# Decoding double-precision weights by one integer addition, with loads in the output weights' space and another opening order

## The chip, the cores and the metric

The kernel runs on one core of a Trainium2 chip. A core has a matrix engine (TensorE, PE in the profile), three engines for elementwise work (VectorE = DVE, ScalarE = ACT, GpSimd = POOL) and a queue that issues the loads and stores (SyncE = SP). Each engine executes its own list of instructions strictly in order; an instruction that waits holds up everything listed behind it on that engine. The metric is the device time of one execution in microseconds (us), the median of several.

## What is computed

Three stages follow one another: a packed attention, a block with softmax-weighted units and a layer norm, and a maximum of three products.

```python
q, k, v: (8, 8, 576, 64)    p: (8, 8, 32, 64)        # batch, heads, tokens, width
p_packed = sm_attn(p, k, v)                          # 32 packs per head
out      = sm_attn(q, p_packed, p_packed)            # tokens attend to the packs
x        = out as (4608 tokens, 512)
h   = x @ w_in                                       # (4608, 1024)
s   = h * softmax(h);   ln = (s - mean) / sqrt(var + 1e-6) * g_ln
x   = ln @ w_out                                     # (4608, 512)
h   = maximum(x @ w1, x @ w2, x @ w3)                # (4608, 768)
out = h @ w_out2                                     # (4608, 512)
```

The matrices w_in, w_out, w1, w2, w3 and w_out2 arrive as 64-bit floating point. The kernel reads each number as two 32-bit words, high and low, and makes a 32-bit float of them on the chip: this is the decoding that the change is about.

## The kernel before

**Tiles.** Tokens go in 36 tiles of 128 (the code's t), and four tiles make a block of 512. The attention of one batch is packed first: its keys are turned and scored against the packs (steps K and s), exponentiated (e), summed and inverted (i), turned (E), and multiplied into the values (p, t). The packed values times w_in give a matrix M of 1024 columns, kept as a high and a low part Mh and Ml (step M, two halves of 512 columns). The queries are turned (Q), and the tokens' shares in the packs are computed in two units per batch (x scores and exponentiates on DVE and ACT, a divides, turns back and splits into ah and al). A tile's h is then ah and al times Mh and Ml: 6 matmuls of 512 columns per half and batch part (steps a and b of `hidden_parts`, lines 649 to 720), followed by a maximum and an exponential (x), the product h * e with its square (c), and the scaling (d). Four such tiles are transposed 128 columns at a time (step T, `y_transpose`) and multiplied by w_out (step y, 6 matmuls per step). Results go to memory, and from about 520 us on the last stage takes them up again. Products of full precision are three matmuls each, of high and low parts.

**Decoding.** `decode` (line 120) works on a raw tile of 512 or 256 numbers per partition. `start` scales the high word on ACT into a scratch tile dt (line 131). `first_half` is two DVE instructions: shift and mask dt (136), and put the sign back into the high word (139). `second_half` is two more on DVE, which cut out the exponent (144) and multiply the low word by it (146), and one addition on POOL (149). There are 8 pieces of w_in, 4 + 8 of w_out (named raw, dt, wt, woh, wol) and 48 of the other matrices, which are decoded along the way, one piece at a time.

**What sets the order.** The opening is written out by hand: the string `st` in `CFG` lists the steps, and `manual_schedule` (line 1117) keeps every engine's list in that order. In it a capital L loads a piece of w_in, 1, 2 and 3 are the three parts of its decoding, o loads a piece of w_out, 4 to 7 are its parts, H0a to H3d are the steps of the first four tiles, and a leading b marks the second batch's steps. From tile 4 on a loop issues steps by the strings s0 to s3, and the program's scheduler interleaves them. Loads wait for the space that they fill: a tile of a pool is taken again only when its last reader is done.

Of the kernel before, what the change touches and what calls it, by code (L numbers as in the profile page):

```python
# [8 lines left out]
F32 = mybir.dt.float32  # L9
# [10 lines left out]
def f32(ap):  # L20
    return ap.bitcast(F32)
# [29 lines left out]
    l0='vv',  # L51
    wr=3,
    l1='v',
# [3 lines left out]
    d0='gggg',  # L57
    fs='g',
    d1='g',
    d2='g',  # L60
# [5 lines left out]
def kernel(  # L66
# [47 lines left out]
    make_identity(nc, ident)  # L114

# [4 lines left out]
    def decode(dst, raw, t, t2=None, add=nc.gpsimd, parts=False):  # L120
# [22 lines left out]
        def second_half():  # L143
            nc.vector.tensor_scalar(t.bitcast(I32), hi, -0x800000, None, op0=ALU.bitwise_and)
            if t2 is None:
                nc.vector.scalar_tensor_tensor(  # L146
                    out=f32(lo), in0=lo.bitcast(U32), scalar=2.0 ** -52, in1=t, op0=ALU.mult, op1=ALU.mult
                )
                add.tensor_tensor(out=dst, in0=f32(hi), in1=f32(lo), op=ALU.add)  # L149
            else:  # L150
                nc.gpsimd.tensor_tensor(out=t, in0=t2, in1=t, op=ALU.mult)
                add.tensor_tensor(out=dst, in0=f32(hi), in1=t, op=ALU.add)
# [32 lines left out]
    woh = big.tile([P, KFF, DM], F32R, name="woh")  # L185
    wol = big.tile([P, KFF, DM], F32R, name="wol")
# [16 lines left out]
    def decode_w_in(c, n):  # L203
        ns = slice(n * 512, (n + 1) * 512)
        raw = wide(words(w_in)[c * P:(c + 1) * P, ns, :])
        t = lt_p.tile([P, TB], F32, tag="ll", name="dt")
        t2 = lt_p.tile([P, TB], F32, tag="lh", name="dt2") if CFG['l0'][n] == 'g' else None
        return [*decode(w_in_sb[:, c, ns], raw, t, t2, parts=True)]
# [4 lines left out]
    def decode_w_out(n, raw):  # L213
# [3 lines left out]
        start, bits, product = decode(wt, raw, t, wt if CFG['l1'] == 'g' else None, ENG[CFG['d1']], parts=True)  # L217
# [23 lines left out]
    def decode_piece(src):  # L241
# [7 lines left out]
        return wt, *decode(wt, raw, t, add=ENG[CFG['d2']])  # L249
# [61 lines left out]

    def split(hi, lo, ps):
        nc.scalar.copy(hi, ps)
        nc.vector.tensor_tensor(out=lo, in0=ps, in1=f32(hi), op=ALU.subtract)
# [27 lines left out]
    class Packed:  # L342
# [145 lines left out]
        def product(self, n):  # L488
# [5 lines left out]
            mp = [bank("mp") for _ in range(NG)]  # L494
# [6 lines left out]
            for g in range(NG):  # L501
                split(Mh[b][:, g, ns], Ml[b][:, g, ns], mp[g])
# [68 lines left out]
        def run(self, what):  # L571
# [3 lines left out]
                K=[self.keys], E=[self.weights], V=[self.values, self.turned_values], M=[self.product], Q=[self.queries],  # L575
# [3 lines left out]
            for x, n in zip(what[::2], what[1::2]):  # L579
                for f in do[x]:  # L580
                    f(int(n))
                self.done.add({'a': 'X'}.get(x, x) + n)
# [4 lines left out]
    class First(Packed):  # L587
# [21 lines left out]
        def room_e1(self, g):  # L609
            if g == 0 or self.b:  # L610
                return super().room_e1(g)
            return [lt_p.tile([P, TB], F32, tag="lh", name="e1")[:, :HALF] for _ in range(2)]

# [423 lines left out]
    def start_step(w):  # L1037
        if w == 'L':
# [295 lines left out]
```

## Time and profile before

| | |
|---|---|
| median of 3 runs | 1087.29 us (1087.15 to 1088.55) |
| the profiled execution | 1090.56 us, of which its span is 1088.8 us |
| PE busy | 1034.7 us, 95% of the span |
| DVE busy | 725.7 us, 67% |
| ACT busy | 475.8 us, 44% |
| POOL busy | 268.0 us, 25% |

An engine's busy share is an average over stages. In the page's table of 40 slices PE is busy 5 to 8 tenths in the first four (27 us each) and 9 tenths in all but one of the rest, so the opening is the place where the matrix engine waits most. The clock that PE is granted has two levels, 1.00 (2.4 GHz) and 0.50 (1.2 GHz); a row between them holds some of both. What ended an idle time is named behind an arrow.

### The profile page before, as it was taken

The numbers are of one execution on the slowest core, as the hardware profiler recorded it, in microseconds if no ns is written. First come the engines' busy times: TensorE is split into PE (matmuls) and PEld (weight loads), VectorE is DVE, ScalarE is ACT, GpSimd is POOL, SyncE is SP. The second block draws the span as 40 slices with busy tenths as digits, with TensorE's granted clock in tenths as the row PEclk, the third lists the DMA queues.
The fourth block names the chain that finished last, engine by engine and source line by source line (L and its number), as shares of the span: only waits on it lengthen the run. The fifth ranks groups of instructions, "written<-read, shape, count | busy, mean of one in ns | idle before, by whom it ended". The sixth has DMA issues, their size and how long they took to land.

```text
span 1088.8 us, 18024 instructions
## 1 busy us (share of the span) xinstructions
PE 1034.7 (95%) x6548; PEld 871.2 (80%) x6548; DVE 725.7 (67%) x1454; ACT 475.8 (44%) x925; POOL 268.0 (25%) x291
## 2 busy tenths in 40 slices
PE   5788999999999999999999999999999999999997
PEld 3355757676777767777899999999989999999996
DVE  5979797878779786764878736725745663672560
ACT  5484867665766666566333421321231142132112
POOL 1214211110212121142577511320140042031002
PEclk9689999999999999999999999999999999999999
DMA  9751537455364643247564644543544453433311
GB/s 270 173 144 57 141 95 207 138 148 158 108 174 118 180 124 106 69 141 240 165 211 165 201 139 123 143 158 116 151 141 146 126 179 120 118 117 125 119 56 59
DMA packets 139464, 154.28 MB, mean 142 GB/s; under 512 B 51824, under 2 KB 92272, under 8 KB 139376
## 3 DMA queue, kind: packets, MB, share of 16 engines
q1 hardware_dynamic: 139376, 153.14, 47.5%
q8 instruction: 52, 0.85, 0.4%
q14 instruction: 36, 0.29, 0.1%
HBM read 116.92 MB, written 36.18 MB: 141 GB/s over the span
## 4 chain that ended last, share of the span: by engine, by line
PE 51%; DVE 2%; issue 1%; POOL 1%; DMA 1%; ACT 1%; DVEq 0%; ACTq 0%; POOLq 0%
PE m L953 32%; PE o L1224 13%; PE y L794 4%; PE h L682 1%; DVE wt L853 1%; DVE r L961 0%; PE tp L765 0%; DVE kept L961 0%; POOL w2l L826 0%; DMA wt<-wdram 0%; DMA wt<-wodram 0%; ACT u L718 0%; POOL hl L1017 0%; POOL t1l L921 0%; DVE t L903 0%
## 5 line engine op out<-in xcount | busy, mean ns | idle before, releaser
L794 PE MATMUL y<-lh,woh 128*128 128x512 f32 x288 | 118.8, 417 | 0.7 <-ACT lh L771 0.7
L794 PE MATMUL y<-ll,woh 128*128 128x512 f32 x288 | 115.8, 402 | 0.2 <-DVE ll L772 0.2
L794 PE MATMUL y<-lh,wol 128*128 128x512 f32 x288 | 114.6, 398 | 0.4 <-POOL wol L222 0.4
L961 DVE TENSOR_TENSOR u<-m,q 128x384 f32<-128x384 f32 x54 | 30.0, 555 | 126.6 <-PE m L953 77.4
L986 ACT COPY q<-m 128x384 f32<-128x384 f32 x54 | 25.9, 480 | 177.4 <-PE m L953 177.4
L1017 POOL TENSOR_TENSOR hl<-cur,hh 128x384 fp32r<-128x384 f32 x36 | 40.7, 1134 | 235.9 <-ACT hh L1016 235.9
L149 POOL TENSOR_TENSOR wt<-raw 128x256 f32<-128x256 f32 (+1 forms) x60 | 39.9, 666 | 238.0 <-DVE raw L146 146.7
L1224 PE MATMUL o<-w2h,hl 128*128 128x512 f32 x216 | 84.4, 391 | 0.6 <-POOL hl L1017 0.6
L1224 PE MATMUL o<-w2l,hh 128*128 128x512 f32 x216 | 84.3, 390 | 0.0
L1224 PE MATMUL o<-w2h,hh 128*128 128x512 f32 x216 | 84.2, 390 | 0.0
L682 PE MATMUL h<-Mh,ah 128*128 128x512 f32 x160 | 67.5, 422 | 1.2 <-ACT ah L568 0.5
L794 PEld LDWEIGHTS y<-lh,woh 128*128 128x128 f32 x288 | 54.1, 189 | 15.9 <-issue 2.7
L682 PE MATMUL h<-Ml,ah 128*128 128x512 f32 x160 | 65.1, 407 | 0.0
L682 PE MATMUL h<-Mh,al 128*128 128x512 f32 x160 | 64.9, 406 | 0.1
L794 PEld LDWEIGHTS y<-lh,wol 128*128 128x128 f32 x288 | 54.4, 189 | 13.0 <-POOL wol L222 0.8
L794 PEld LDWEIGHTS y<-ll,woh 128*128 128x128 f32 x288 | 54.7, 190 | 12.0 <-issue 1.4
L953 PE MATMUL m<-t2h,s 128*128 128x384 f32 x216 | 64.2, 337 | 0.0
L953 PE MATMUL m<-b22h,s 128*128 128x384 f32 x216 | 63.6, 335 | 0.0
L953 PE MATMUL m<-t1h,s 128*128 128x384 f32 x216 | 63.5, 334 | 0.0
L953 PE MATMUL m<-t3h,s 128*128 128x384 f32 x216 | 63.5, 334 | 0.0
L772 DVE SCALAR_TENSOR_TENSOR ll<-tp,g_sb,lh 128x512 fp32r<-128x512 f32 x72 | 52.3, 743 | 14.4 <-ACT lh L771 14.2
L961 DVE TENSOR_TENSOR kept<-r,kept 128x384 f32<-128x384 f32 x72 | 58.1, 807 | 2.4
(199 smaller groups left out, 2723.7 us busy)
## 6 DMA issues: line engine op xcount, KB each, us to landing
s<-sdram SPq DMA_DIRECT2D x188, 256.0 KB, 2.9
kt<-in_k_dram SPq DMA_DIRECT2D x16, 576.0 KB, 5.3
vt<-in_v_dram SPq DMA_DIRECT2D x16, 576.0 KB, 4.7
ydram<-yt SPq DMA_DIRECT2D x36, 256.0 KB, 2.8
raw<-in_moe_w_dram SPq DMA_DIRECT2D x36, 256.0 KB, 2.8
b<-ydram SPq DMA_DIRECT2D x24, 384.0 KB, 4.5
out_dram<-ob SPq DMA_DIRECT2D x36, 256.0 KB, 2.4
sdram<-s SPq DMA_DIRECT2D x28, 256.0 KB, 2.1
```

The source lines that it names most:

```text
L149: add.tensor_tensor(out=dst, in0=f32(hi), in1=f32(lo), op=ALU.add)
L682: nc.tensor.matmul(at['h'][:, n, :], lhsT=x, rhs=m[:, g, n * 512:(n + 1) * 512], start=(i == 0), stop=(i == len(ops()) - 1),)
L772: last[nc.vector] = nc.vector.scalar_tensor_tensor(out=ll, in0=tp, scalar=gc, in1=f32(lh), op0=ALU.mult, op1=ALU.subtract)
L794: nc.tensor.matmul(ys[half][m], lhsT=w[:, kc, ms], rhs=x, start=(kc == 0 and i == 0), stop=(kc == KFF - 1 and i == 2),)
L853: nc.vector.tensor_tensor(out=out, in0=x, in1=y, op=op)
L953: nc.tensor.matmul(out, lhsT=w, rhs=y, start=start and i == 0, stop=i == len(ops) - 1, skip_group_check=not start,)
L961: mark[0] = nc.vector.tensor_tensor(**what)
L986: mark[1] = nc.scalar.copy(q, ba)
L1017: nc.gpsimd.tensor_tensor(out=hl, in0=t, in1=f32(hh), op=ALU.subtract)
L1224: nc.tensor.matmul(ops[i], lhsT=x[:, ts], rhs=w, start=(c == 0 and n == 0), stop=(c == KF2 - 1 and n == 2),)
```

## The change

Four things change. `decode` now has ACT round the low word: it scales the low word by 2^-29, adds 2^23 (a new constant tile `ulps`) and writes an integer, which is the three bits to be added and one step of the exponent. POOL then adds the two words as integers. The two DVE instructions of `second_half` are gone, and every decoded number is twice its value. The factors are taken back where they cost no instruction more, except one of 8 columns on POOL: M is copied with a factor 0.5 on ACT and the low part is one fused DVE instruction, and g_ln is multiplied by 0.125 (step g).

The values of the first batch and the last two raw pieces of w_in no longer wait for a buffer: they land in two tiles (`early`) that later become woh and wol (step W takes them over). The list `st` is another one. The attention of batch 0 now comes before any decoding, tile 0's first half stands before the queries' second half, and most of the second batch's steps come after the fourth tile. What stands behind the bar in the list is issued outside the hand-written schedule. M is split in two steps, n (product and high part) and m (low part).

```diff
@@ decode @@
         def start():
             nc.scalar.activation(t, f32(hi), AF.Copy, scale=2.0 ** -112)
-            if t2 is not None:
-                nc.scalar.activation(t2, lo.bitcast(U32), AF.Copy, scale=2.0 ** -52)
+            nc.scalar.activation(lo, lo.bitcast(U32), AF.Identity, bias=ulps, scale=2.0 ** -29)
...
         def second_half():
-            nc.vector.tensor_scalar(t.bitcast(I32), hi, -0x800000, None, op0=ALU.bitwise_and)
-            if t2 is None:
-                nc.vector.scalar_tensor_tensor(
-                    out=f32(lo), in0=lo.bitcast(U32), scalar=2.0 ** -52, in1=t, op0=ALU.mult, op1=ALU.mult
-                )
-                add.tensor_tensor(out=dst, in0=f32(hi), in1=f32(lo), op=ALU.add)
...
+            nc.gpsimd.tensor_tensor(out=dst.bitcast(I32), in0=hi, in1=lo, op=ALU.add)
@@ tiles @@
-    woh = big.tile([P, KFF, DM], F32R, name="woh")
-    wol = big.tile([P, KFF, DM], F32R, name="wol")
+    woh = wol = None
+    early = [big.tile([P, KFF * DM], F32, tag=x, name="early") for x in ("woh", "wol")]
@@ decode_w_in @@
-        raw = wide(words(w_in)[c * P:(c + 1) * P, ns, :])
+        src, i = words(w_in)[c * P:(c + 1) * P, ns, :], 4 * n + c - 6
+        if i < 0:
+            raw = wide(src)
+        else:
+            raw = early[0].bitcast(I32)[:, i * DFF:(i + 1) * DFF].rearrange("r (f t) -> r f t", t=2)
+            nc.sync.dma_start(out=raw, in_=src)
@@ product @@
             for g in range(NG):
-                split(Mh[b][:, g, ns], Ml[b][:, g, ns], mp[g])
+                nc.scalar.activation(Mh[b][:, g, ns], mp[g], AF.Copy, scale=0.5)
+
+        def product_low(self, n):
...
+                nc.vector.scalar_tensor_tensor(
+                    out=Ml[b][:, g, ns], in0=self.mp[g], scalar=0.5, in1=f32(Mh[b][:, g, ns]),
+                    op0=ALU.mult, op1=ALU.subtract,
+                )
@@ First @@
+        def load_v(self, g):
...
+            n = 4 * KJ * D
+            self.vt[g] = early[1][:KP, g * n:(g + 1) * n].rearrange("r (h x) -> r h x", h=4)
+            nc.sync.dma_start(out=self.vt[g], in_=v[self.b, 4 * g:4 * g + 4].rearrange("h (r j) d -> r h (j d)", j=KJ))
@@ start_step @@
+        if w == 'W':
+            woh, wol = (big.tile([P, KFF, DM], F32R, tag=x, name=x) for x in ("woh", "wol"))
+        elif w == 'g':
+            nc.gpsimd.tensor_scalar_mul(g_sb, g_sb, 0.125)
@@ the list @@
-        'k0 k1 L L L L K0 1 s0 e0 K1 v0 v1 q0 L L 2 3 L 1 i0 E0 2 3 L q1 G o bk0 bk1 o s1 1 e1 E1 2 3 i1 1 1 p0 p1 2 3 2 3 t0 t1 1 1 Q0 2 3 2 3 '
+        'k0 k1 v0 v1 q0 L L L L L L L L q1 G K0 s0 K1 s1 e0 i0 E0 e1 i1 E1 p0 t0 p1 t1 Q0 1 2 3 1 x0 2 3 1 1 2 3 2 3 1 o bk0 bk1 o 1 a0 2 3 n0 1 m0 H0a 2 3 1 2 3 Q1 2 3 4 x1 H1a '
-        for w in CFG['st'].split():
+        for w in CFG['st'].split('|')[0].split():
             start_step(w)
+    for w in CFG['st'].split('|')[1].split():
+        start_step(w)
```

Three places show the move. The first is ACT's list in the opening, from the first batch's last steps to the shares of its tokens. Here e is the exponential, ppz and ppT the packed values, qT the turned queries, dt the first scratch tile of a decoding, raw the raw words and x the tokens' scores. Before:

```order
L437 ACTIVATE e_301,se_302<-s_286,m_295 128x288
L308 COPY e1T<-tp 96x384 x2
L131 ACTIVATE dt<-raw 128x512 x2
L475 ACTIVATE ppz<-pv,rim 128x64 x4
L308 COPY ppT<-tp 128x128 x2
L131 ACTIVATE dt<-raw 128x512 x2
L308 COPY qT<-tp 128x4x128 x2
L131 ACTIVATE dt<-raw 128x512
L542 ACTIVATE x<-x 128x2x256
L313 CAST Mh<-mp 128x512 x2
```

And now:

```order
L463 ACTIVATE ppz<-pv,rim 128x64 x2
L300 COPY ppT<-tp 128x128
L300 COPY qT<-tp 128x4x128 x2
L128 ACTIVATE dt<-raw 128x512
L129 ACTIVATE raw<-raw,ulps 128x512
L128 ACTIVATE dt<-raw 128x512
L129 ACTIVATE raw<-raw,ulps 128x512
L539 ACTIVATE x<-x 128x2x256
L128 ACTIVATE dt<-raw 128x512
L129 ACTIVATE raw<-raw,ulps 128x512
L128 ACTIVATE dt<-raw 128x512
L129 ACTIVATE raw<-raw,ulps 128x512
```

Before, seven starts of a decoding stand ahead of the copies to qT, four of them in these rows; now none does, and behind the copies each piece has two instructions.

The second place is PE's list from the turned queries to the first products of a tile. Here qu and qtail are raw queries, st the scores, mp the product for M, and h a tile's product. Before:

```order
L640 MATMUL tp<-ident,qu 128x128 x8
L530 MATMUL st<-qT,ppT 32x256 x8
L497 MATMUL mp<-w_in_sb,ppT 32x512 x8
L640 MATMUL tp<-ident,qu 128x128 x8
L647 MATMUL tp<-ident,qtail 128x128 x2
L530 MATMUL st<-qT,ppT 32x320 x8
L497 MATMUL mp<-w_in_sb,ppT 32x512 x8
L682 MATMUL h<-Mh,ah 128x512
L682 MATMUL h<-Ml,ah 128x512
L682 MATMUL h<-Mh,al 128x512
```

And now:

```order
L644 MATMUL tp<-ident,qu 128x128 x8
L527 MATMUL st<-qT,ppT 32x256 x8
L485 MATMUL mp<-w_in_sb,ppT 32x512 x8
L686 MATMUL h<-Mh,ah 128x512
L686 MATMUL h<-Ml,ah 128x512
L686 MATMUL h<-Mh,al 128x512
L686 MATMUL h<-Mh,ah 128x512
L686 MATMUL h<-Ml,ah 128x512
L686 MATMUL h<-Mh,al 128x512
L644 MATMUL tp<-ident,qu 128x128 x8
L651 MATMUL tp<-ident,qtail 128x128 x2
L527 MATMUL st<-qT,ppT 32x320 x8
```

The six products of tile 0's first half now stand ahead of the second half of the queries, of the second unit's scores and of the second product for M.

The third place is PE's list around the first transpose of u, the scaled tiles, behind the fourth tile's last product. Here s, e, pv, kt and ppz belong to the second batch's packing, and y is the product with w_out. Before:

```order
L466 MATMUL pv<-vt,e1T 32x64 x24
L682 MATMUL h<-Mh,ah 128x512
L682 MATMUL h<-Ml,ah 128x512
L682 MATMUL h<-Mh,al 128x512
L485 MATMUL tp<-ident,ppz 128x128
L640 MATMUL tp<-ident,qu 128x128 x8
L647 MATMUL tp<-ident,qtail 128x128 x2
L455 MATMUL tp<-ident,e_808 96x128 x6
L765 MATMUL tp<-ident,u 128x128 x4
L466 MATMUL pv<-vt,e1T 32x64 x24
L765 MATMUL tp<-ident,u 128x128 x4
L485 MATMUL tp<-ident,ppz 128x128
```

And now:

```order
L408 MATMUL s_688<-kT,pT 32x288 x4
L408 MATMUL s_689<-kT,pT 32x288 x4
L443 MATMUL tp<-ident,e_707 96x128 x6
L769 MATMUL tp<-ident,u 128x128 x8
L393 MATMUL tp<-ident,p_sb 128x128
L399 MATMUL tp<-ident,kt 128x96 x3
L798 MATMUL y_839<-lh,woh 128x512
L798 MATMUL y_840<-lh,woh 128x512
L399 MATMUL tp<-ident,kt 128x96 x9
L769 MATMUL tp<-ident,u 128x128 x4
L408 MATMUL s_797<-kT,pT 32x288 x4
L408 MATMUL s_798<-kT,pT 32x288 x4
```

Before, the second batch's packing was nearly through at the first transpose of u. Now one group's scores stand ahead of it, and the other group's keys, scores and both groups' values follow it, between the products y.

## Rows read from the trace of the kernel before

**Rows 1.** Stretches: us, PE, PEld, DVE, ACT, POOL busy, clock, DMA share, GB/s

```profile
0.00:42.40 42.40, 23.37 (x251) 13.43 (x251) 29.95 (x58) 19.38 (x46) 9.71 (x19) 0.78 0.93 244
51.00:76.20 25.20, 19.43 (x172) 12.99 (x170) 20.34 (x51) 23.47 (x49) 4.93 (x5) 0.97 0.44 113
84.00:108.70 24.70, 21.29 (x149) 11.62 (x149) 24.66 (x50) 12.24 (x25) 10.71 (x11) 1.00 0.19 57
108.70:520.00 411.30, 394.61 (x2907) 292.75 (x2906) 317.35 (x770) 272.11 (x528) 79.47 (x113) 1.00 0.50 144
```

**Rows 2.** Timeline of the opening, all engines: start us, us, instruction

```profile
11.87 0.42 DVE L136 TENSOR_SCALAR dt<-dt 128x512 int32<-128x512 int32 x1
12.32 0.69 DVE L139 SCALAR_TENSOR_TENSOR raw<-raw,dt 128x512 int32<-128x512 int32 x1
...
28.65 1.11 PE L530 MATMUL st<-qT,ppT 64*32 64x256 f32 x16 [2.40 <-ACT qT L308]
...
33.33 0.77 DVE L536 STREAM_TRANSPOSE x<-st 128x256 f32<-128x256 f32 x2
...
37.78 1.28 DVE L314 TENSOR_TENSOR Ml<-mp,Mh 128x512 fp32r<-128x512 f32 x2
...
40.91 0.77 DVE L567 STREAM_TRANSPOSE y<-x 128x256 f32<-128x256 f32 x2
...
42.39 0.80 PE L682 MATMUL h<-Mh,ah 128*128 128x512 f32 x1 [0.49 <-ACT ah L568]
```

**Rows 3.** Groups of instructions by form, whole program: count, busy us, mean ns

```profile
L149 POOL TENSOR_TENSOR wt<-raw 128x256 f32<-128x256 f32 x56 | 35.7, 638 | 220.5 <-DVE raw L146 138.0 <-issue 20.4 <-DVE powers L710 15.1
...
L131 ACT ACTIVATE dt<-raw 128x256 f32<-128x256 f32 x56 | 24.7, 442 | 31.4 <-DMA raw<-in_moe_w_dram 15.3 <-DVE raw L146 12.2 <-DMA raw<-in_moe_w_out_dram 3.6
...
L131 ACT ACTIVATE dt<-raw 128x512 f32<-128x512 f32 x12 | 8.1, 679 | 3.1 <-DMA raw<-in_moe_w_in_dram 3.1
```

**Rows 4.** Timeline, PE: two products of h at either clock

```profile
44.33 0.63 PE L682 MATMUL h<-Mh,ah 128*128 128x512 f32 x1
...
44.76 0.63 PE L682 MATMUL h<-Ml,ah 128*128 128x512 f32 x1
...
50.52 0.39 PE L682 MATMUL h<-Ml,ah 128*128 128x512 f32 x1
...
50.75 0.39 PE L682 MATMUL h<-Mh,al 128*128 128x512 f32 x1
```

**Rows 5.** Timeline: a tile's normalisation, and the first transpose of u

```profile
50.09 1.19 DVE L690 TENSOR_REDUCE nm<-h 128x1 f32<-128x1024 f32 x1
...
51.38 1.11 ACT L692 ACTIVATE u<-h,nm 128x1024 f32<-128x1024 f32 x1 [0.44 <-DVE nm L690]
...
54.93 1.15 ACT L703 ACTIVATE spare<-u,nmu 128x1024 bf16<-128x1024 f32 x1 [0.99 <-DVE nmu L701]
...
74.87 1.24 ACT L718 ACTIVATE u<-u,nmu,powers 128x1024 f32<-128x1024 f32 x1
...
76.16 0.48 PE L765 MATMUL tp<-ident,u 128*128 128x128 f32 x1 [2.77 <-ACT u L718]
```

**Rows 6.** Stretch around that transpose, columns as in the first group

```profile
75.00:78.00 3.00, 1.84 (x49) 1.45 (x49) 0.93 (x3) 1.80 (x2) 0.30 (x2) 0.50 0.66 186
```

**Rows 7.** The same stretch for line 144, then line 146, alone: DVE busy

```profile
84.00:108.70 24.70, 1.53 (x5) 1.00 0.19 57
...
84.00:108.70 24.70, 3.51 (x5) 1.00 0.19 57
```

**Rows 8.** Waits of PE, 108.7 to 520 us: us in total, times, longest

```profile
PE tp L485 <- DVE ppz L477: 4.9, 7, 1.5
PE tp L765 <- ACT u L718: 2.4, 3, 1.4
...
PE st L530 <- DVE powers L710: 0.2, 1, 0.2
PE tp L455 <- ACT e L437: 0.2, 1, 0.2
```

More of the change, by code (lines that the diff above doesn't have):

```diff
@@ L50 @@
     pre=1,
-    l0='vv',
     wr=3,
-    l1='v',
     he=[1, 3],
@@ L114 @@
     make_identity(nc, ident)
+    ulps = const.tile([P, 1], F32, name="ulps")
+    nc.gpsimd.memset(ulps, 2.0 ** 23)
     ENG = {'v': nc.vector, 'g': nc.gpsimd}
@@ L118, with decode @@
     ENGINES = {'A': ET.Activation, 'D': ET.DVE, 'P': ET.PE, 'G': ET.Pool, 'S': ET.SP}
-    def decode(dst, raw, t, t2=None, add=nc.gpsimd, parts=False):
+    def decode(dst, raw, t, parts=False):
         lo, hi = raw[:, :, 0], raw[:, :, 1]
@@ L204, in decode_w_in @@
         ns = slice(n * 512, (n + 1) * 512)
-        raw = wide(words(w_in)[c * P:(c + 1) * P, ns, :])
+        src, i = words(w_in)[c * P:(c + 1) * P, ns, :], 4 * n + c - 6
[4 more added lines that the diff above has]
+            nc.sync.dma_start(out=raw, in_=src)
         t = lt_p.tile([P, TB], F32, tag="ll", name="dt")
-        t2 = lt_p.tile([P, TB], F32, tag="lh", name="dt2") if CFG['l0'][n] == 'g' else None
-        return [*decode(w_in_sb[:, c, ns], raw, t, t2, parts=True)]
+        return [*decode(w_in_sb[:, c, ns], raw, t, parts=True)]
     HM = DM // 2
@@ L216, in decode_w_out @@
         wt = lt_p.tile([P, TB], F32, tag="ll", name="wt")
-        start, bits, product = decode(wt, raw, t, wt if CFG['l1'] == 'g' else None, ENG[CFG['d1']], parts=True)
+        start, bits, product = decode(wt, raw, t, parts=True)
         def words_of():
@@ L248, in decode_piece @@
         wt = dec_p.tile([P, DC], F32, tag="wt", name="wt", bufs=1)
-        return wt, *decode(wt, raw, t, add=ENG[CFG['d2']])
+        return wt, *decode(wt, raw, t)
     held, spot = [], [None]
@@ L310, in ev @@
             nc.vector.tensor_copy(out, in_)
-    def split(hi, lo, ps):
-        nc.scalar.copy(hi, ps)
-        nc.vector.tensor_tensor(out=lo, in0=ps, in1=f32(hi), op=ALU.subtract)
     def bank(name):
@@ L493, in product @@
             ns = slice(n * 512, (n + 1) * 512)
-            mp = [bank("mp") for _ in range(NG)]
+            mp = self.mp = [bank("mp") for _ in range(NG)]
             for h in range(H):
@@ L501, in product @@
             for g in range(NG):
-                split(Mh[b][:, g, ns], Ml[b][:, g, ns], mp[g])
+                nc.scalar.activation(Mh[b][:, g, ns], mp[g], AF.Copy, scale=0.5)
+        def product_low(self, n):
+            b = self.b
+            ns = slice(n * 512, (n + 1) * 512)
+            for g in range(NG):
+                nc.vector.scalar_tensor_tensor(
+                    out=Ml[b][:, g, ns], in0=self.mp[g], scalar=0.5, in1=f32(Mh[b][:, g, ns]),
+                    op0=ALU.mult, op1=ALU.subtract,
+                )
         def queries(self, c):
@@ L574, in run @@
                 s=[self.scores], e=[self.powers], i=[self.inverses], x=[self.tokens], a=[self.shares],
-                K=[self.keys], E=[self.weights], V=[self.values, self.turned_values], M=[self.product], Q=[self.queries],
+                K=[self.keys], E=[self.weights], V=[self.values, self.turned_values], M=[self.product, self.product_low], n=[self.product], m=[self.product_low], Q=[self.queries],
                 p=[self.values], t=[self.turned_values],
@@ L581, in run @@
                     f(int(n))
-                self.done.add({'a': 'X'}.get(x, x) + n)
+                self.done.add({'a': 'X', 'm': 'M'}.get(x, x) + n)
         def steps(self):
```

11 lines of the change are left out of this document (4 added, 7 removed), and 4 rows, old and new, of the table st.

## The prediction

> **What bounds the kernel now.** I read the table of stretches first, then the timeline of the opening, then the waits of PE. The stretches show three regimes [rows 1]. To 42.4 us PE is busy 23.37 of 42.4 us at a mean clock of 0.78: nothing dense can start until the first shares are there. From 51 to 76.2 ACT is busy 23.47 of 25.2 us, with the exponentials and scalings of the first four tiles, and PE idles 5.8 us. From 84 to 108.7 DVE is busy 24.66 of 24.7 us and PE idles 3.4 us. Behind that PE is the bound: from 108.7 to 520 us it is busy 394.61 of 411.3 us and idles 16.7. So a change of the opening and of DVE's work can win only out of these idle times and out of time at the lower clock; the last stage, from 520 us, holds no decoding and stays as it is.
>
> **The change part by part.**
>
> First, the prices of a decoded piece. Off DVE go lines 144 and 146. From 84 to 108.7 us five of each take 1.53 and 3.51 us [rows 7], so about 1.0 us per piece in a mixture of sizes, 5.0 us of a stretch that DVE fills. ACT gets a second instruction per piece, which no row shows, since it reads and writes integers and adds a bias. Its nearest row is the first one, 0.442 us for 256 numbers and 0.679 for 512 [rows 3]. I take the same; it can't well be under that, having the same elements to pass, and the exponential with a bias takes 1.11 us for 1024 [rows 5], so over 0.7 for 512 would surprise me. That makes 56 x 0.442 + 12 x 0.679 = 33 us more on ACT. POOL adds integers where it added floats, at 0.638 us for 256 [rows 3]. I take that price again; were it twice as dear, 56 x 0.638 = 36 us would come onto an engine that is busy 79.47 of 411.3 us [rows 1], so it would lengthen only a piece's own way. The factor 0.5 rides on instructions that stand anyway; the 8 columns of g_ln are needed at the first transposes only and stand in a gap of POOL. These two cost nothing, and would cost under 1 us if the gap were gone.
>
> Second, the opening up to tile 1. Loads: p, both groups' keys and values and half the queries are 3.0 MB, 12 us at 244 GB/s [rows 1], so they are there by about 15 us, with the start-up of some 3 us; the values are wanted at about 19, in a chain that ACT and PE run without decoding. In the kernel before, the scores of the first unit start at 28.65 [rows 2], behind seven starts of a decoding on ACT, 7 x 0.68 = 4.8 us, part of it in time that ACT would have waited. I take 3.6 off: 25.0. From there DVE has four pieces of w_in at 0.42 + 0.69 = 1.1 us [rows 2], and the unit's own work. This is read from the way from 33.33 to 41.68 (40.91 + 0.77): 8.35 us, less a piece with four instructions (2.2) and the pair at 37.78 (1.28), so 4.9 [rows 2]. With 1.1 for the scores' first matmuls and the first start on ACT, and 0.4 of waits on ACT between, that is 25.0 + 0.9 + 4.4 + 4.9 + 0.5 = 35.7. A cast and the first copy of M (0.6 each) follow: tile 0's first product starts at 37.0 instead of 42.39 [rows 2].
>
> That lead of 5.4 us is lost at once. The second half of the queries, the second unit's scores and the second product for M now stand behind these six products (6 x 0.43 at the lower clock [rows 4] = 2.6, so 39.6). They need 4.3 us on PE with their copies, to 43.9; the unit's DVE work and its exponential 6.5, to 50.4; and only then DVE makes the low part of M's second half, 0.65 each. The second product of H0b waits for it at 51.1. Eleven products at 0.23 [rows 4] end at 53.8, where the kernel before ends its last one at 51.0. Term 1: **+2.8 us**.
>
> Third, the norms of tiles 0 to 3. The first maximum starts at 52.5 instead of 50.09 [rows 5]. ACT then has, per tile, 1.11 + 1.15 + 1.24 us [rows 5] and two reads of 0.19: 15.6 us for four, and between them a cast, one piece's two instructions and the first keys, 3.6. Together 19.2 from 53.8, and 1.3 of waits for DVE's maxima: the last scaling ends at 74.3, where it ended at 76.1. It is faster since six steps of the second batch have gone from ACT's list here. But two exponentials (1.1 us) and a transpose of theirs now stand ahead of the first transpose of u: 76.4 against 76.16 [rows 5]. Term 2: **-2.6 us**, which leaves +0.2.
>
> Fourth, from that transpose to the end of tile 4's products, 32.5 us before (to 108.7). PE has 7.4 us more to do in it: keys, scores, values and queries that it did from 51 to 76.2 within its 19.43 busy us [rows 1]. It has 3.4 us of idle time for them in the second part, and 7.8 us at a mean clock of about 0.66 in the first. DVE loses 5.0 and gains 2.5 with the second batch's small steps, so some 30 us. ACT has about 30 too, with the second batch's copies and thirteen pieces' second instructions. Three engines with about 30 us each in lists that wait for one another: I take 32.3, so a gain of 0.2, and the bounds are 30 (nothing waits) and 36.5 (PE's 7.4 us find room for the 3.4 only). Term 3: **-0.2 us**. By tile 4 the two kernels stand level.
>
> Fifth, the rest of the first stages. PE's waits of 108.7 to 520 us are put down to DVE for 9.3 us (nine rows, from 4.9 to 0.2) and to ACT for 6.9 (eight rows, from 2.4 to 0.2) [rows 8]. DVE is busy 317.35 of 411.3 us there and loses up to 1.0 us for each of some 53 pieces, so 77% become 65 to 67%; ACT goes from 272.11 to about 295, 66 to 72% [rows 1]. I take half of DVE's waits away and add a quarter to ACT's: -4.7 + 1.7. The bounds are -9.3 (all of DVE's waits go) and +3 (ACT's grow by half, and DVE's were waits for a chain, not for a busy engine). Term 4: **-3.0 us**.
>
> Sum: 2.8 - 2.6 - 0.2 - 3.0 = -3.0. The profiled execution took 1090.56 us (span 1088.8 and 1.76 around it), 3.3 above the median of 1087.29. So 1087.6 for such an execution, and **1084.3** against the median.
>
> **A rule to weigh.** In the kernel before PE has little to do from 73 us until the transpose at 76.16, and the stretch from 75 to 78 is at 0.50, the lower level [rows 5, 6]. The changed list has PE without work twice: between the end of H1b (53.8) and the moment at which tile 0's bank comes free (57.4), and again after H3b. The Trainium skill ("TensorE: Matmul & The Clock Gate", Part 1) says that the default state is throttled and that activity releases it. The row above agrees. By the rule the twelve products of tile 2 would run at 1.2 GHz; if the clock holds, the sum stays, if not, the third rival's first part, 2.4 us, comes on top of it and gives 1086.7.
>
> **The rivals.**
>
> 1. The cover is larger: all of DVE's 9.3 us of waits go [rows 8], and the stretch to tile 4 shrinks by DVE's 2.5 us net. For it: DVE is full there and PE is not. Against it: ACT takes 33 us in its place. 2.8 - 2.6 - 2.5 - 9.3 = -11.6: 1075.7.
>
> 2. No net effect: ACT gives back what DVE wins. For it: ACT already bounds 51 to 76.2 [rows 1], and PE's waits for it are nearly as long as those for DVE. Term 4 is then 0: 1087.3.
>
> 3. Slower, by what was pushed behind the fourth tile. PE stands still after H1b, its clock falls, and tile 2's twelve products cost 0.43 instead of 0.23 each, +2.4, on the way to the norms, so the first transpose comes at 78.6 or so. Then the 7.4 us of the second batch's packing find only the 3.4 us of idle time, +4.0. With term 4 at -1 the sum is 0.2 + 2.4 + 4.0 - 1 = +5.6: 1092.9. It decides from the point at which the stretch from the first transpose of u to tile 4's end takes more than 35 us. For it: the row at 0.50 and PE busy 7.8 of 7.8 us just behind that transpose; against it: DVE's relief in that stretch.
>
> That the change doesn't do what it says is a small case, an integer addition on POOL that takes twice as long; it lies within the second and third.
>
> **How the numbers follow.** The forecast, -1 to -6 us, has 0.42; the first rival 0.16, the second 0.20, the third 0.22. A measurement of this kernel can tell 0.2%, 2.2 us, from no change. Faster by more than that: the third of the forecast's cases nearest to zero is left out partly, 0.33, and the first rival's 0.16, so 0.49. The same: 0.09 of the forecast, 0.17 of the second rival and 0.01 of the third, 0.27. Slower: 0.21 and 0.03, so 0.24. The likeliest case's own range is 1081 to 1087. The range over the cases goes from 1075 (the first rival) to 1094 (the third, with a bound of 1 us more), and leaves out the ends of both.
>
> **What would show it.** Right: the first product of h at 36 to 38 us and the last of tile 1 at 53 to 55; the first transpose of u at 75 to 78; tile 4's last product at 107 to 111; DVE busy some 65% and ACT some 72% from there to 520 us, and PE's waits for ppz and the low parts shorter, with an idle time of 12 to 15 instead of 16.7 us. Wrong: the second instruction on ACT well over 0.7 us for 512 numbers, or POOL's addition over 1.1; a clock of 0.50 between 57 and 63; PE's waits for copies on ACT grown to more than 10 us; or the dense products starting no earlier than 42, which would say that loads, not the order, bound the opening.

## The result, and the profile after

The changed kernel is slower: 1.0106 times the time of before (interval 1.0081 to 1.0131); the medians of eleven runs each are 1101.72 and 1088.26 us. The forecast was 1084.3, and the range ended at 1094. The changed kernel's runs go from 1096.74 to 1104.42 us, those of before from 1087.15 to 1096.02.

The profiled execution took 1099.66 us, 9.1 more than that of before, where the means of all runs differ by 11.6. The chain of stages splits this up (starts and ends from the timelines of both):

| until | before | after | gained or lost in the stretch | forecast |
|---|---|---|---|---|
| tile 1's last product ends | 51.1 | 57.5 | +6.4 | +2.8 |
| first transpose of u behind the fourth norm | 76.2 | 80.6 | -2.0 | -2.6 |
| tile 4's last product ends | 108.8 | 117.3 | +4.1 | -0.2 |
| last transpose of u starts | 519.1 | 526.9 | -0.7 | -3.0 |
| end of the span | 1088.8 | 1097.9 | +1.3 | 0 |

The stretches of the changed kernel, with the columns of [rows 1], and two short ones behind tile 1:

```profile
0.00:42.40 42.40, 28.41 (x221) 14.38 (x222) 17.68 (x36) 23.42 (x51) 7.72 (x18) 1.00 0.93 247
51.00:76.20 25.20, 16.97 (x70) 12.29 (x70) 16.42 (x35) 15.47 (x28) 5.10 (x5) 0.80 0.13 39
57.00:60.60 3.60, 0.53 (x3) 0.09 (x1) 3.53 (x7) 2.33 (x4) 1.04 (x1) 0.87 0.04 8
60.60:66.40 5.80, 5.74 (x14) 4.51 (x15) 2.10 (x8) 3.69 (x6) 0.00 (x0) 0.50 0.25 85
84.00:108.70 24.70, 21.37 (x261) 13.72 (x260) 20.06 (x42) 18.62 (x44) 10.07 (x12) 1.00 0.40 109
108.70:520.00 411.30, 395.68 (x2915) 292.77 (x2914) 281.80 (x669) 287.94 (x578) 75.59 (x111) 1.00 0.50 138
```

DVE has what the change promised: 17.68 instead of 29.95 us in the opening, 20.06 instead of 24.66 from 84 us, 281.80 instead of 317.35 behind it. PE won little from that: its idle time behind 108.7 us is 15.6 us, where it was 16.7. From 51 to 76.2 us no engine is full any more; they wait for one another. The fourth row is at 0.50, the lower clock, just behind the third, in which PE did 0.53 us of work.

The timeline of PE in the opening, answering to [rows 2, 4, 5] (start us, us, instruction, wait before it):

```profile
26.55 1.11 PE L527 MATMUL st<-qT,ppT 64*32 64x256 f32 x16 [0.68 <-ACT qT L300]
...
39.63 0.50 PE L686 MATMUL h<-Mh,ah 128*128 128x512 f32 x1 [1.08 <-ACT Mh L490]
...
53.42 0.80 PE L686 MATMUL h<-Ml,ah 128*128 128x512 f32 x1 [2.83 <-DVE Ml L496]
54.01 0.63 PE L686 MATMUL h<-Mh,al 128*128 128x512 f32 x1
54.44 0.63 PE L686 MATMUL h<-Mh,ah 128*128 128x512 f32 x1
...
57.14 0.40 PE L686 MATMUL h<-Mh,al 128*128 128x512 f32 x1
60.66 0.77 PE L686 MATMUL h<-Mh,ah 128*128 128x512 f32 x1 [3.13 <-DVE u L701]
...
66.35 0.47 PE L686 MATMUL h<-Ml,ah 128*128 128x512 f32 x1
...
80.55 1.91 PE L769 MATMUL tp<-ident,u 128*128 128x128 f32 x8
```

Twice PE waits about 3 us (2.83 for the low part of M's second half, 3.13 for tile 0's bank), and behind either wait products start 0.43 us apart instead of 0.23, six of them behind the first and fourteen behind the second. The prices, from the groups by form (count, busy us, mean ns), answering to [rows 3]:

```profile
L129 ACT ACTIVATE raw<-raw,ulps 128x256 int32<-128x256 uint32 x56 | 29.4, 536 | 9.3 <-DMA raw<-in_moe_w_dram 7.0 <-DMA raw<-in_moe_w_out_dram 2.3
...
L129 ACT ACTIVATE raw<-raw,ulps 128x512 int32<-128x512 uint32 x10 | 7.7, 771 | 0.0
...
L140 POOL TENSOR_TENSOR wt<-raw 128x256 int32<-128x256 int32 x56 | 36.3, 648 | 187.2 <-DVE raw L135 80.2 <-DMA wdram<-wt 34.3 <-ACT raw L129 22.2
```

ACT's second instruction is about 0.09 us dearer than the first one at either size; POOL's integer addition costs what its float addition did. And PE's waits from 108.7 to 520 us (total, times, longest), answering to [rows 8], and behind them the row of before that answers to the first:

```profile
PE tp L399 <- ACT pT L300: 4.6, 6, 1.2
PE tp L769 <- ACT u L722: 2.3, 2, 1.4
PE tp L769 <- DVE x L533: 2.2, 1, 2.2
PE tp L473 <- DVE ppz L465: 1.8, 4, 0.8
```

```profile
PE tp L411 <- ACT pT L308: 0.3, 1, 0.3
```

The wait for ppz has shrunk from 4.9 to 1.8 us, and a wait for ACT's copy pT, the turned packs, that had been 0.3 is now 4.6. All waits put down to DVE are 6.9 us, where they were 9.3; all those put down to ACT are 8.3, where they were 6.9.

### The profile page after: what moved, and what is told of

It reads as the page before. It is cut to its first block, busy times and chain, and to the rows that moved or that the text cites. A ratio compares the mean times of both kernels' runs of the same rounds, so it can differ in the third digit from the quotient of the medians.

```text
span 1097.9 us, 17988 instructions
## 1 busy us (share of the span) xinstructions
PE 1040.2 (95%) x6548; PEld 874.3 (80%) x6548; DVE 678.0 (62%) x1318; ACT 504.8 (46%) x993; POOL 268.3 (24%) x293
## 3 DMA queue, kind: packets, MB, share of 16 engines
q1 hardware_dynamic: 139376, 153.14, 47.6%
## 4 chain that ended last, share of the span: by engine, by line
PE 50%; DVE 2%; issue 1%; DMA 1%; POOL 1%; ACT 1%; DVEq 0%; ACTq 0%; POOLq 0%
PE m L957 32%; PE o L1235 12%; PE y L798 4%; PE h L686 1%; DVE wt L857 1%; DMA out_dram<-ob 1%; DVE r L965 0%; PE tp L769 0%; DVE kept L965 0%; POOL w2l L830 0%; DMA wt<-wodram 0%; DMA wt<-wdram 0%; ACT ob L1244 0%; ACT u L722 0%; POOL hl L1021 0%
## 5 line engine op out<-in xcount | busy, mean ns | idle before, releaser
L140 POOL TENSOR_TENSOR wt<-raw 128x256 int32<-128x256 int32 (+1 forms) x60 | 40.4, 674 | 193.1 <-DVE raw L135 80.2
```

The lines of the kernel that those rows point to most:

```text
L140: nc.gpsimd.tensor_tensor(out=dst.bitcast(I32), in0=hi, in1=lo, op=ALU.add)
```

## The experiments

Each kernel is compared with the kernel before on the same chip. Starts of a tile's first maximum are from the timelines of the profiled executions; ratios have their 95% interval.

| | ratio to before | tile 0 | tile 4 | tile 16 | tile 22 | tile 35 |
|---|---|---|---|---|---|---|
| before | 1 | 50.1 | 109.6 | 266.9 | 347.9 | 501.0 |
| changed | 1.0106 (1.0081 to 1.0131) | 56.0 | 117.3 | 272.2 | 356.9 | 508.8 |
| e1 decoding alone | 1.0007 (0.9994 to 1.0019) | 47.3 | 109.1 | 263.8 | 348.5 | 500.2 |
| e2 order alone | 1.0176 (1.0154 to 1.0197) | 64.3 | 126.8 | 282.0 | 362.6 | 515.3 |
| e3 changed, decoded earlier | 1.0087 (1.0067 to 1.0108) | 54.0 | 114.8 | 268.1 | 353.3 | 505.2 |
| e4 changed, packing back | 1.0058 (1.0038 to 1.0079) | 56.7 | 109.4 | 266.6 | 352.2 | 503.9 |
| e5 changed, M's low part first | 1.0119 (1.0105 to 1.0133) | 55.1 | 117.9 | 275.6 | 360.1 | 511.9 |
| e6 changed, gap filled | 1.0044 (1.0031 to 1.0058) | 56.2 | 115.6 | 268.2 | 351.4 | 503.3 |
| e7 e1, a piece later | 1.0007 (0.9989 to 1.0025) | 47.5 | 108.3 | 262.7 | 347.2 | 499.7 |
| e8 e1, gap filled | 0.9988 (0.9979 to 0.9997) | 47.7 | 108.2 | 263.6 | 346.8 | 498.5 |
| e9 before, gap filled | 0.9975 (0.9962 to 0.9987) | 49.8 | 107.3 | 262.8 | 343.7 | 496.3 |
| e10 e8, second filling | 1.0015 (1.0002 to 1.0028) | 46.9 | 109.3 | 263.1 | 348.4 | 500.3 |
| e11 e1, late pieces old | 1.0005 (0.9988 to 1.0022) | 47.5 | 107.8 | 264.6 | 345.5 | 498.0 |
| e12 changed, e3 and three fillings | 1.0058 (1.0036 to 1.0080) | 54.4 | 112.1 | 269.7 | 353.7 | 506.5 |
| e13 e11, gap filled | 0.9962 (0.9946 to 0.9978) | 47.4 | 105.5 | 265.8 | 346.3 | 498.7 |
| e14 e4, late pieces old | 0.9981 (0.9964 to 0.9998) | 56.2 | 109.8 | 264.2 | 344.9 | 497.3 |

**e1, the decoding alone.** The changed kernel's `decode` and factors; the list of before (with the step g), every piece through `wide`, the values loaded as before.

> The new decoding alone (with its factors 0.5 and 0.125); the order, the landing of the values and of the raw pieces are those of before. Theory L (the new order costs the time, the decoding wins some): H0a starts at 38 to 40 us, since four DVE instructions for each piece become two, tile 4 ends by 106, and the time is 1081 to 1086. Theory A (the second instruction on ACT costs the time): PE's waits for ACT grow beyond 108.7 us, and the time is 1090 or more. In the prediction's terms: its fourth term alone says 3.0 us less from tile 4's end to the last transpose.

Neither: 1.0007. PE's waits for ACT grow from 6.9 to 9.7 us, as theory A has it, but those for DVE fall from 9.3 to 5.1. The opening is 2.75 us ahead at tile 0 and all but level at tile 4 (0.5). Where the lead goes is seen in PE's timeline and in the stretch behind it:

```profile
91.91 1.11 PE L758 MATMUL tp<-ident,u 128*128 128x128 f32 x4 [3.70 <-DVE Ml L489]
```

```profile
92.00:100.00 8.00, 8.00 (x42) 3.21 (x43) 5.42 (x10) 4.45 (x11) 1.62 (x2) 0.50 0.10 35
```

A wait of 3.70 us, and eight microseconds at the lower clock behind it.

**e2, the order and the landing places with the old decoding.** `decode` with its four DVE instructions again, factors 1.

> The new order and the new landing places with the old decoding (four DVE instructions a piece, one on ACT, a float addition on POOL). Theory L: slower than the changed kernel, 1100 to 1108, H0a starting at 43 or later, since DVE has four more instructions' worth in the same crowded stretch. Theory A: 1090 or less.

As theory L has it: order and landing places cost 1.76% with the old decoding, and with the new one they make the step from e1's 1.0007 to 1.0106. So the decoding is worth 0.7% in the changed order and nothing in the old one.

**e3, earlier decoding.**

```diff
- E0 e1 i1 E1 p0 t0 p1 t1 Q0 1 2 3 1 x0 2 3 1 1 2 3 2 3 1 o ..
+ E0 1 2 3 e1 i1 E1 p0 1 2 3 t0 p1 1 2 3 t1 Q0 1 x0 2 3 1 o ..
```

> The changed kernel, with three of the eight pieces of w_in decoded before the first query transposes, in the stretch from 15 to 26 us in which DVE stood idle for 8.5 us, and one less while the first unit's shares wait. Theory O (the opening is late because the list starts decoding only at 26.4 us): H0a starts at 35.5 to 37.5 instead of 39.63, tile 1 ends at 54 to 55 instead of 57.5, and the time falls by 2 to 4 us against the changed kernel. Rival: the chain of the second unit sets the end of tile 1, so H0a comes earlier and tile 1's end does not; time unchanged within 1 us.

Theory O in the trace: tile 0 starts at 37.32, tile 1 ends at 55.7 (54 to 55 was expected), the last maximum is 3.6 us earlier. The ratio falls by 0.19%, with overlapping intervals, so that a gain in time is not shown. The wait for M's low part stays (2.89 us).

**e4, the packing back.** From tile 1 on the list of before; the values, the pieces of w_in and the bar in the list stay as changed.

```diff
- H0x g 5 6 H1x H0c H1c H0d H2a H2b H2x 7 ..  H3d | be0 bE0 ..
+ H0x g 5 bK0 bv0 H0c H1x H0d bs0 H2a H2b be0 H1c H2x bE0 .. H3d bi1 | Y T ..
```

> The changed kernel up to tile 1, and then the order of before: the second batch's keys, scores, weights, values and queries stand among tiles 0 to 3 again. Theory P (the third rival: PE idles behind tile 1 and falls to the lower clock, and the packing pushed behind tile 3 finds no room): tile 2's products at 0.23 us each instead of 0.43, from tile 1's end to tile 4's end 56 to 58 us instead of 59.6, time 2 to 4 us less than the changed kernel. Rival: ACT's list gets longer by the same copies ahead of the norms, the first dense transpose comes later, and the stretch stays 59 us or more.

Theory P, and more than it asked for: tile 2's products start 0.23 us apart (the stretch 61 to 67 is at 1.00), tile 1's end is even later than in the changed kernel (58.9), and yet tile 4 is level with before:

```profile
61.25 0.50 PE L684 MATMUL h<-Mh,ah 128*128 128x512 f32 x1
61.59 0.39 PE L684 MATMUL h<-Ml,ah 128*128 128x512 f32 x1
61.82 0.39 PE L684 MATMUL h<-Mh,al 128*128 128x512 f32 x1
```

So a late tile 1 is made good by tile 4 if the packing stands among the first tiles. What ties tile 4 to the packing is that it holds tokens of both batches, 24 products instead of 12, and needs both parts of M for the second batch. These are the last instructions of the low part in the kernel before, in the changed one and in e4:

```profile
102.18 0.65 DVE L314 TENSOR_TENSOR Ml<-mp,Mh 128x512 fp32r<-128x512 f32 x1
```

```profile
110.09 0.65 DVE L496 SCALAR_TENSOR_TENSOR Ml<-mp,Mh 128x512 fp32r<-128x512 f32 x1
```

```profile
101.63 0.65 DVE L494 SCALAR_TENSOR_TENSOR Ml<-mp,Mh 128x512 fp32r<-128x512 f32 x1
```

The second batch's packing starts on PE at 50.98, 68.99 and 58.70 us in these three. The landing places and the bar, which this kernel keeps, show no cost up to tile 4. Between tiles 16 and 22 it loses 4.6 us against before all the same; e14 returns to that.

**e5, M's low part first.** `n1 W a1 m1` becomes `n1 W m1 a1`.

> The changed kernel, with the low part of M's second half ahead of the second unit's shares in the list. Theory O (tile 1 is late because DVE makes that low part only behind the unit's whole softmax, at 52.72 us, and PE waits 2.83 us and then runs eight products at 0.43 us): the wait is gone, tile 1 ends at 53.5 to 55 instead of 57.5, and the time falls by 2 to 4 us against the changed kernel. Rival: the shares come 1.3 us later in exchange and tiles 2 and 3 wait for them, time within 1 us.

The rival in its number, not in its mechanism. Tile 1 ends 2.3 us earlier, and the time doesn't fall. Tile 2 waits not for the shares but for the bank of tile 0, as in the changed kernel; PE only stands still longer, and all of tile 2 runs at the lower clock, as it did there:

```profile
54.59 0.63 PE L684 MATMUL h<-Mh,al 128*128 128x512 f32 x1
60.98 0.77 PE L684 MATMUL h<-Mh,ah 128*128 128x512 f32 x1 [5.76 <-DVE u L699]
```

**e6, the gap filled.** A step behind H1b:

```diff
+ z = bank("idle")
+ for _ in range(26): nc.tensor.transpose(z[:, :P], ident, ident)
```

> The changed kernel, with 26 transposes of the identity into an otherwise unused bank behind tile 1's last product, so that PE is busy for some 3 us of the 3.13 in which it stands still there (their result is read by nobody). Theory C (the lower clock behind that gap is what costs): tile 2's products run at 0.23 us each, its twelfth ends at 63.5 instead of 66.1, and the time falls by 2 to 3 us. Rival: the norms on ACT and DVE set the first dense transpose anyway; it stays at 80.5 and the time within 1 us.

Theory C, and more time than it asked for. Every engine's list is otherwise the same. The filling and what follows it, from the timeline and from the stretches:

```profile
58.20 3.00 PE L1057 MATMUL idle<-ident 128*128 128x128 f32 x26
60.95 0.48 PE L684 MATMUL h<-Mh,ah 128*128 128x512 f32 x1
61.27 0.39 PE L684 MATMUL h<-Ml,ah 128*128 128x512 f32 x1
61.50 0.40 PE L684 MATMUL h<-Mh,al 128*128 128x512 f32 x1
```

```profile
61.00:66.40 5.40, 5.40 (x25) 4.37 (x24) 3.31 (x10) 4.66 (x7) 0.00 (x0) 1.00 0.24 89
```

From 1.0106 to 1.0044 for 26 useless transposes. The twelve products of tile 2 take 3.0 instead of 5.5 us, and the first transpose of u comes at 78.42 instead of 80.55. At tile 4 the trace is 1.7 us ahead of the changed kernel's; another 3.8 are won between tile 4 and tile 35, with the same lists. Of these, 1.3 are one wait for a unit's scores, in the changed kernel and here:

```profile
152.74 1.80 PE L769 MATMUL tp<-ident,u 128*128 128x128 f32 x12 [2.17 <-DVE x L533]
```

```profile
149.79 1.79 PE L767 MATMUL tp<-ident,u 128*128 128x128 f32 x12 [0.94 <-DVE x L531]
```

The waits for pT are 1.1 us less in total. Why the same lists run closer here, the traces don't tell, and nothing shows that the clock did it. In e5, again with the same lists there but for two steps in the opening, this wait is longer, and the clock falls behind it:

```profile
153.61 2.25 PE L767 MATMUL tp<-ident,u 128*128 128x128 f32 x12 [2.47 <-DVE x L531]
```

```profile
156.00:160.00 4.00, 4.00 (x14) 1.82 (x6) 3.46 (x6) 2.95 (x6) 0.25 (x2) 0.50 0.52 130
```

**e7, a piece later.** In e1, ACT's exponential of the second batch stood behind a piece of w_out whose load it awaited for 1.90 us; the piece is held back until M's copies are issued.

> The decoding alone (the first experiment's kernel), with ACT's first two instructions for the fourth late piece of w_out moved behind the copies of M for the second batch: in the first experiment they stood ahead of the second unit's exponential and waited 1.90 us for a load, and PE then 3.70 us for M's low part, and ran at the lower clock until 100 us. Theory C: PE's wait there falls to 2 us or less, the clock stays at its upper level, tile 4 ends at 104 to 106 instead of 108.4, and the time falls to 1084 to 1086. Rival: the load was not what ACT's list needed, DVE's chain of the softmax sets the copies; PE's wait stays over 3 us and the time within 1 us of the first experiment's 1089.

The rival in its number: PE's wait is 3.58 us, the ratio unchanged. The instruction that ACT then waits with is the next one in its list:

```profile
88.03 0.40 ACT L227 CAST woh<-wt 128x256 fp32r<-128x256 f32 x1 [1.89 <-POOL wt L138]
88.34 0.73 ACT L539 ACTIVATE x<-x 128x640 f32<-128x640 f32 x1
```

**e8 and e9, the wait for tile 3's norm filled**, in the decoding alone and in the kernel before:

```diff
  for i in range(TB // P):
+     if (j, kc) == (0, 0) and i == 3: idle(26)
```

> The decoding alone, with 26 transposes of the identity between the third and the fourth transpose of the first group, where PE waits 2.76 us for tile 3's norm, so that the clock does not fall there (their result is read by nobody). Theory C: the six products behind it take 0.23 instead of 0.43 us, and the stretch from 76 to 84 us is at 1.00 instead of 0.75; the time falls by 1 to 2 us. Rival: what PE gains it waits for again at 88 us, where M's low part comes when DVE's list lets it; time the same within 1 us.

> The kernel before, with 26 transposes of the identity (read by nobody) between the third and the fourth transpose of the first group, where PE waits 2.77 us for tile 3's norm. Theory C (what the eighth experiment won is the clock, whatever the decoding): the stretch from 76 to 84 us is at 1.00 instead of 0.65, the first products of y at 0.23 us, and the time falls by 1 to 2.5 us to some 1086. Rival (the decoding won it, the filling only let it show): the time stays within 1 us of 1088, since DVE, full from 84 to 108.7 us in this kernel, takes the lead back.

Theory C for both. The stretch that was at 0.65 in the kernel before is at 1.00 in e9; before and after the filling:

```profile
76.00:84.00 8.00, 7.84 (x75) 6.33 (x76) 2.96 (x8) 3.58 (x7) 1.59 (x3) 0.65 0.65 200
```

```profile
76.00:84.00 8.00, 7.70 (x93) 5.54 (x82) 5.10 (x13) 4.51 (x9) 2.21 (x3) 1.00 0.56 159
```

e8 wins 0.19% on e1, with intervals that just overlap, and e9 0.25% on before, with an interval below 1. The new decoding was not needed for it.

**e10, a second filling in e8.** 34 more ahead of the wait at 88 us.

> The eighth experiment's kernel, with 34 more such transposes ahead of the group of transposes that waits 3.70 us at 88 us for the low part of M (six of them are issued earlier, behind the first filling). Theory C: the clock stays at its upper level from 92 to 98 us, tile 4's products end 1.5 to 2.5 us earlier, and the time falls to 1084 to 1085.5. Rival: the softmax of the second batch on DVE and ACT sets tile 4 there, so its end stays, and the time is within 1 us of 1087.

Neither; it lost 0.27%. PE's next waits came behind the filling, and its clock fell a little later:

```profile
92.58 1.26 PE L520 MATMUL st<-qT,ppT 64*32 64x256 f32 x16 [1.27 <-DVE Ml L489]
...
97.21 1.95 PE L478 MATMUL mp<-w_in_sb,ppT 64*32 64x512 f32 x12 [2.33 <-DVE ll L774]
```

A filling moves the list behind it too. In these runs one filled wait paid (e6, e8, e9), and a second one behind it did not.

**e11, the late pieces decoded as before**, in e1.

> The decoding alone, but with the old four DVE instructions for the 56 late pieces of 256 numbers (their values come out smaller by a power of two, since nothing else is adapted, so that the output differs). It takes the relief of DVE back behind the opening. Theory S (second rival: in the late stretch ACT gives back what DVE wins): from the start of tile 4's norm to that of tile 35's 391 us as in the first experiment and before, DVE busy again some 315 us, PE's waits for ppz back at 4 to 5 us and those for pT back under 1; time 1087 to 1090. Rival (the fourth term of the prediction): that stretch is 3 us longer than in the first experiment, 394, and the time 1091 to 1093.

Theory S in its waits, though those for ppz come back to 3.0 us and not to 4 or 5; those for pT are gone:

```profile
PE tp L474 <- DVE ppz L466: 3.0, 6, 1.0
...
PE tp L400 <- ACT pT L301: 0.3, 1, 0.3
```

The wait for pT tells the late decoding apart: it is 0.3 us in every kernel with the old one and 2.2 to 4.6 in every one with the new. That for ppz does not, since e2 has 1.8 with the old decoding.

Tiles 4 to 35 take 390.3 us (e1: 391.1, before: 391.4). That the whole stretch stays the same hides two opposite parts. Tiles 16 to 22 take 80.5 to 81.1 us in every kernel with the old late decoding (before, e2, e9, e11) and 83.2 to 85.6 in every one with the new. One such place, ACT's and then PE's timeline of the changed kernel:

```profile
301.87 0.44 ACT L128 ACTIVATE dt<-raw 128x256 f32<-128x256 f32 x1 [1.68 <-DMA raw<-in_moe_w_out_dram]
302.21 0.52 ACT L129 ACTIVATE raw<-raw,ulps 128x256 int32<-128x256 uint32 x1
302.73 1.15 ACT L707 ACTIVATE spare<-u,nmu 128x1024 bf16<-128x1024 f32 x1
303.78 0.19 ACT L707 ACTIVATION_READ_ACCUMULATOR spare<-u,nmu 128x1 f32 x1
303.87 0.24 ACT L300 COPY pT<-tp 128x128 f32<-128x128 f32 x1
...
304.17 0.47 PE L399 MATMUL tp<-ident,kt 96*128 96x96 f32 x3 [1.22 <-ACT pT L300]
```

ACT waits for a load with the decoding at the head of its list, and the copy for which PE stands still is queued behind. In the kernel before, the piece at this place finds its words landed:

```profile
292.75 0.42 ACT L131 ACTIVATE dt<-raw 128x256 f32<-128x256 f32 x1
```

Waiting for loads is nothing new for ACT: it did so ahead of the starts of the decoding before, too [rows 3]. But the late pieces also stand closer together now: between the first maxima of tiles 16 and 22 POOL adds up 16 of them in nearly every kernel with the new late decoding, and 11 in every one with the old. How much of the loss is due to that and how much to ACT's second instruction was not separated.

**e12, the changed kernel with e3's list and three fillings** (behind M's first product of the second half, behind tile 1, and ahead of the second batch's weights).

> The changed kernel with the earlier decoding of the third experiment and three fillings of 26 transposes of the identity: behind the first product of M's second half, where PE waits 2.83 us, behind tile 1's last product, and ahead of the transposes of the second batch's weights, where it waits 3.38 us. Theory C (the changed order loses by the clock in its three gaps, and by its late decoding): tile 1 ends at 54 us, tile 2's products run at 0.23, the stretch from 76 to 84 is at 1.00, tile 4 ends at 110 to 112, and the time is 1088 to 1091. Rival: the packing pushed behind tile 3 still finds no room, and the time stays above 1093.

The opening does most of what theory C says: tile 4's maximum at 112.1 instead of 117.3, the stretch from 76 to 84 us at 1.00, though tile 1 ends at 55.8 and not at 54. The time doesn't (a median of 1095.4, the rival's side): tiles 16 to 22 take 84.0 us, 3.5 more than in e2, and tiles 4 to 16 take 157.6. It is no better than e6 with its one filling.

**e13 and e14, the new decoding for the opening alone**: in the order of before with the filling, and in e4.

```diff
- decode_piece(words(w)[r0:r0 + P, f:f + DC, :])
+ decode_piece(words(w)[r0:r0 + P, f:f + DC, :], late=True)
```

> The order of before; the new decoding for w_in and w_out, the old four DVE instructions for the 48 pieces behind them (with a factor of 0.5 instead of 0.125 on g_ln, so that the product is the same); 26 transposes of the identity where PE waits for tile 3's norm. Theory S (the new decoding wins in the opening and loses in tiles 16 to 22 what it wins elsewhere): tiles 16 to 22 take 81 us, tile 4's maximum comes at 107 to 108, and the time is 1083 to 1085.5, ratio under 0.9975. Rival (the opening's lead is always lost by tile 4, as in the first experiment): the time is that of the ninth experiment, ratio 0.9975, or worse.

> The fourth experiment's kernel (the changed one with the second batch's packing among tiles 0 to 3 again), with the old decoding for the 48 late pieces. Theory S: tiles 16 to 22 take 81 instead of 85.6 us, and the time falls by 2 to 4 us to a ratio of 1.002 to 1.004 or less. Rival (the late loss comes from the order or the landing places): it stays at 1.005 or more.

Theory S in both: tiles 16 to 22 take 80.5 and 80.7 us. e14 falls from e4's 1.0058 to 0.9981, twice what was expected; 4.9 us of it lie between tiles 16 and 22, and the traces have another 2.8 between tiles 4 and 16. So with the packing back and the old late decoding the changed kernel's whole loss is gone, its landing places and its opening up to tile 1 kept. e13, at 0.9962, has the lowest ratio of all, though its interval overlaps that of e9; its profiled execution, the one in the table, is the longest of its twelve.

## Why the prediction was wrong

**Term 1, the opening to tile 1: +2.8 forecast, +6.4 measured.** "tile 0's first product starts at 37.0" was 2.6 us early. Of these, 1.55 were lost by the start of the first scores, at 26.55 instead of 25.0 (the sum writes 0.9 and 0.5 where the terms ahead of it are 1.1 and 0.4, which is 0.1 us). And the list begins to decode only behind the first query copies (26.39 us), and DVE, idle for 8.47 us until then, makes the pieces inside the first unit's softmax. e3 shows that the order decides: with three pieces decoded ahead of the queries tile 0's first product starts at 37.32, though the first scores start later still, at 28.60. "The second product of H0b waits for it at 51.1" was the right wait, 2.3 us early. "Eleven products at 0.23" then left out that PE stands still ahead of them and runs the first six of them at the lower clock: they take 4.1 us instead of 2.7.

**Term 2, the norms: -2.6 forecast, -2.0 measured.** Near in size, but partly by luck: the stretch holds 2.1 us of the lower clock behind tile 1, which e6 takes out of it and the term did not contain. Without them it would be about -4.1.

**Term 3, from there to tile 4: -0.2 forecast, +4.1 measured.** This is the step that failed in kind. It weighed three engines with some 30 us of work each, and let PE's packing find room in PE's idle time and in DVE's relief. The stretch, before and after:

```profile
76.20:108.80 32.60, 29.19 (x223) 18.01 (x224) 27.73 (x57) 15.70 (x31) 12.27 (x14) 0.92 0.31 92
```

```profile
80.60:117.30 36.70, 33.00 (x329) 22.58 (x328) 28.94 (x62) 26.51 (x62) 15.77 (x18) 0.96 0.42 117
```

DVE is no longer near full and ACT is not either, yet PE's idle time has not shrunk: 3.7 us, where it was 3.4. Nearly all of it are waits for the second batch's own steps, 1.05 us for ppz, 1.57 for its scores, 0.57 for M's low part and 0.33 for the keys. So PE's 3.8 us more of work and the 4.1 us more of the stretch go together. What the runs show in the prediction's place is that the packing has to stand where PE idles anyway, among the first tiles: tile 4 needs it, and it now starts 18 us later; the low part of the second batch's M ends 7.9 us later, and tile 4's last product 8.5. With the list of before from tile 1 on (e4), tile 4 comes 8 us earlier than in the changed kernel, though tile 1 ends later. That run restores the whole list behind tile 1, not the packing alone. Wherever the packing stands among the first tiles, tile 4's maximum is at 105.5 to 109.8 us, whether tile 1 ends at 47.6 or at 58.9; wherever it stands behind the third tile, at 112.1 or later. So a sum that carries the opening's lead on to tile 4 failed as well: e1's lead is lost by then, and e4's lag is made good.

This is the third rival's second part, which had "against it: DVE's relief in that stretch", and the point from which that rival decides was 35 us. Its first part, the clock, had the right size: the twelve products of tile 2 are 2.4 us shorter in e6, and 2.4 were forecast; they count in term 2's stretch. The Trainium skill ("TensorE: Matmul & The Clock Gate", Part 1) says that the default state is throttled and activity releases it. The runs agree: just behind the gap the clock is at 0.50, and with the gap filled at 1.00.

**Term 4, from tile 4 to the last transpose: -3.0 forecast, -0.7 measured** (+0.1 between the maxima of tiles 4 and 35). It came out as the second rival had it: ACT gives back what DVE wins. Of "I take half of DVE's waits away and add a quarter to ACT's" the second half held: ACT's went up by 1.4 us, with 1.7 forecast. The first was mis-sized: DVE's went down by 2.4 and not by 4.7, since a wait of 2.2 us for a unit's scores (DVE x) stands beside the shorter ones for ppz. In e1, without the new order, it is the other way round: DVE's go down by 4.2, and ACT's up by 2.8, near the bound of 3. With the old late decoding tiles 16 to 22 are 3.8 us shorter in e11 than in e1, and 4.9 shorter in e14 than in e4. From tile 4 to tile 35 that leaves 0.8 us in the order of before and 7.0 in that of e4.

**The last stage: 0 forecast, +1.3.** It shows one wait of 1.4 us for a copy of the output on ACT, which the kernel before does not have; it was not followed up.

The prices were near: 0.536 and 0.771 us for ACT's second instruction, where 0.442 and 0.679 were taken and over 0.7 would have surprised, together some 6 us more on an engine that was not full.

What stays open is why tiles 4 to 16 take between 152.5 us (e6) and 157.7 (e5) with the same lists, beyond the one wait that e6 shows and the clock behind it, and why single executions of either kernel differ by 8 to 9 us. The landing places alone were not run; e4, which keeps them, is level with before at tile 4, and e14 is no slower at the end.

## What to carry to other kernels

A step moved out of a stretch where PE also waits takes PE's cover with it: count the wait, and the lower clock behind it, before the work that was moved. An engine that is full in a stretch need not be what the stretch waits for; look at what stands at the head of the list of the engine that takes over the work, above all if that instruction waits for a load. Before adding up stretches, ask what the last instructions of each one need: here tile 4 needs the second batch's packing, and what had been won or lost at tile 1 was gone by then. Where a wait of PE is fixed and about 3 us long, useless transposes of the same length are a cheap try (0.25% in the kernel before, 0.6% in the changed one), but not ahead of a wait that can shift (e10).

## What was not expected of the hardware

26 transposes in a gap of 3.13 us were worth 2.1 us up to the end of the next twelve products, and the ratio fell by 0.62%, some 6.7 us; that the rest, too, is the clock's price was not shown. A wait of 2.47 us was followed by products at the lower clock in e5, where one of 2.17 us at the same place in the changed kernel was not. And ACT's conversion of integers with a bias and scale took 0.536 us for 256 numbers, 1.2 times its plain scaling of floats.
